# First MoE's second product for two token tiles at once, and a third weight matrix scaled by ScalarE

## The chip, the core and the metric

One core of one Trainium2 chip. The metric is the device time of one launch in microseconds (us), the median of three runs; less is better.

## What is computed

Attention with a bias made from positions, a first MoE layer on its output, and a second MoE layer on that. The reference, cut to what matters here:

```python
x = attention(q, k, v, bias)             # 4 batches, 8 heads, 576 tokens, 64 per head
x = x.transpose(0, 2, 1, 3).reshape(2304, 512)
# first MoE: w_in 512 x 1024, w_out 1024 x 512
h = x @ w_in
solu = h * softmax(h)
ln = (solu - mean(solu)) / sqrt(var(solu) + 1e-6) * g_ln
x = ln @ w_out
# second MoE: w_gate, w_val 512 x 1536, w_out 1536 x 512
out = (sigmoid(x @ w_gate) * (x @ w_val)) @ w_out
```

Inputs come in 8 bytes a number and are decoded on the chip (`decode`). Nearly every product is made of three fp16 products: each factor is split into a high part and a rest (hi, lo), and hi x hi, hi x lo and lo x hi are added up.

## The kernel before

The 2304 tokens are 18 tiles of 128. Attention runs in 72 ticks (`a_qk`, `a_soft`, `a_split`, `a_pv`, `a_x`, `a_xt`): a tick's scores are L553 and L558, its softmax L577 to L596, its transposition a DMA on SP's queue (L601), its product with the values L620. Between ticks the loop over `t` takes up to three items of `side_work`, and from a certain point those come from `moe_items` (L891): for each tile i four quarter-products with w_in (`m_g1`, L767, hps), the softmax and norm (`m_ew1`, `m_ew2`), for the tile before it the transposition into `lt` with its evictions on ScalarE (L812) and VectorE (L813) (`m_ew3`), and four items `m_g2(i - 1, dc)`, dc 0 to 3, for the second product: 24 matmuls of 128 columns each (L824, x2ps <- lt, w1f), weights being a 128 x 128 block of w_out. The item of dc = 3 also evicts the sum (L829 on ScalarE, L830 on VectorE) and stores a tile of 256 KB into the DRAM scratch `x2_d` through SP (L832, x_d <- x). A tile's items may begin only once attention is through with its tokens (`ready`). TensorE's order from `open_moe` to the end of attention is the order of the code (`manual_schedule`); the other engines', and TensorE's later, come from a scheduler with priorities.

After the last tick the rest of the first MoE is interleaved with the second MoE's weights. The weights are units in a list: `w2_dec` loads 512 KB through SP (`load_w`, L690, wraw, three buffers), decodes on VectorE (L184, L185, L188) and squares on ScalarE; `w2_scale(jc)` and `w2_scale_out` make the scales (the latter's out-scale is L1148 and L1150); `w2_split` scales the matrix (L695 on GpSimd, w2tmp <- w2f, sw), takes the high part (L698, ScalarE) and the rest (L699 on GpSimd, w2f <- w2tmp, w2f). Twelve splits of the third matrix (mat 2, w_out) stand behind the out-scale. `load_x2` brings x2 back in groups of 4, 2, 4, 4 and 4 tiles (L1191, xb <- x_d).

Group 0 is computed plainly: `gate_val` for twelve column blocks j makes s_ps (L1342, 512 columns), ScalarE's sigmoid, VectorE's gate product (L1348, fr <- s_ps, fr) and the split of the result for fp16 (L1209 on ScalarE and L1210 on VectorE, gv); `second_out` (L1372, ops) needs gv of all twelve blocks. Group 1 does the same with 256 columns. The last three groups use sums of weight blocks and of x2 blocks (`w2_sums`, `x2_sums`, VectorE's L1228 through the helper `add`, 126 in all, and L1231 on ScalarE) and seven products in place of eight (`seven`, `gate_val7`, prod L1304).

The functions that the change touches:

Of the kernel before, what the change touches and what calls it, by code (L numbers as in the profile page):

```python
# [41 lines left out]
NP = 4  # L42
NP16 = 3
NPT = 4
NLT = 2
SPLIT = 0
NGB = 2
GB_ACT = (0,)
# [1 line left out]
W2A = 12  # L50
W2B = 10
W2P = 0
NHT = 2
NET = 0
TAILQ = 1
BD = 2
# [46 lines left out]
def attn_moe_kernel(  # L103
# [7 lines left out]
    act, dve, pool, pe, sp = nc.scalar, nc.vector, nc.gpsimd, nc.tensor, nc.sync  # L111
# [8 lines left out]

    dram = enter(ctx, "scratch", 1, space=DRAM)
    bias_d = dram.tile([5, 128, H, 640], F32, name="bias_d")
    x2_d = dram.tile([18, 128, 4, 2, 128], F16, name="x2_d")

    const = enter(ctx, "const")
    sm0 = enter(ctx, "sm0", 1)
# [77 lines left out]
    def ring(nm, shape, dt, tag=None):  # L204
        r = rings[nm]
        n = turn.get(nm, 0) % len(r)
        turn[nm] = n + 1
        return r[n].tile(shape, dt, name=nm, tag=tag or nm)
# [481 lines left out]
        sp.dma_start(out=raw.rearrange("p f t -> p (f t)"), in_=src[rows, cols].bitcast(I32))  # L690
        return raw

    def split_w(w, s_, hi, lo, tmp, eng=None):
        if eng is None:
            pool.tensor_scalar(out=tmp, in0=w, scalar1=s_, scalar2=0.0, op0=ALU.mult, op1=ALU.add)  # L695
        else:
            act.activation(out=tmp, in_=w, func=ACTF.Copy, scale=s_)
        act.activation(out=hi, in_=tmp, func=ACTF.Copy)  # L698
        (eng or pool).tensor_tensor(out=lo, in0=tmp, in1=hi, op=ALU.subtract)  # L699
# [103 lines left out]
    def m_ew3(i):  # L803
        mo.pop((i, "m"))
        e = mo.pop((i, "e"))
        lt = glob["lt"].tile([128, 2, 8, 128], F16, name="lt")
        for n in range(2):
            tp = ps_m.tile([128, 4, 128], F32, name="ltp", tag="m")
            for f in range(4):
                pe.transpose(tp[:, f], e[:, 512 * n + 128 * f:512 * n + 128 * f + 128], id_sb)  # L810
            hi = lt[:, 0, 4 * n:4 * n + 4]
            act.activation(out=hi, in_=tp, func=ACTF.Copy)  # L812
            dve.tensor_tensor(out=lt[:, 1, 4 * n:4 * n + 4], in0=tp, in1=hi, op=ALU.subtract)  # L813
        mo[i, "lt"] = lt

    def m_g2(i, dc):
        lt = mo[i, "lt"]
        if dc == 0:
            mo[i, "x2"] = ps_m.tile([128, 4, 128], F32, name="x2ps", tag="m")
        ps = mo[i, "x2"]  # L820
        n = 0
        for f in range(8):
            for (wl, ll) in ((0, 0), (0, 1), (1, 0)):
                pe.matmul(ps[:, dc], wout16[:, f, wl, 128 * dc:128 * dc + 128], lt[:, ll, f],  # L824
                          start=(n == 0), stop=(n == 23))
                n += 1
        if dc == 3:
            x2 = glob["x2"].tile([128, 4, 2, 128], F16, name="x2")
            act.activation(out=x2[:, :, 0], in_=ps, func=ACTF.Copy, scale=2.0 ** -15)  # L829
            dve.scalar_tensor_tensor(out=x2[:, :, 1], in0=ps, scalar=2.0 ** -15, in1=x2[:, :, 0],  # L830
                                     op0=ALU.mult, op1=ALU.subtract)
            glob["st"] = sp.dma_start(out=x2_d[i], in_=x2)  # L832
            mo.pop((i, "lt"))
            mo.pop((i, "x2"))


    ticks, tiles, ready = [], [], []
# [51 lines left out]
            when(u, lambda bb=bb, hp=hp, prep=prep: prep(bb, hp), at if nm == "v" else late)  # L889

    def moe_items():  # L891
        for i in range(19):
            if i < 18:
                for n in range(2):
                    for half in range(2):
                        yield ready[i] + LAG_PV + LAG_X + 1, (lambda i=i, n=n, half=half: m_g1(i, n, half))
                yield 0, (lambda i=i: m_ew1(i))
            if i >= 1:
                yield 0, (lambda i=i: m_ew3(i - 1))
            if i < 18:  # L900
                yield 0, (lambda i=i: m_ew2(i))
            if i >= 1:
                for dc in range(4):
                    yield 0, (lambda i=i, dc=dc: m_g2(i - 1, dc))


    xt_p = {0: enter(att_x, "xt0", 2, "right")}
# [103 lines left out]
    def open_moe():  # L1011
        st.close()
        ms = glob["s"] = ExitStack()
        xt_p[1], xt_p["M"] = enter(m1, "xt1", 2), enter(m1, "xtm", 1)
        glob.update((nm, enter(ms, nm, bufs)) for nm, bufs in
                    (("e", 2), ("hs", 1), ("lt", NLT), ("x2", 1), ("ms", 4)))
        grow("p", NP - NP0)
        grow("p16", NP16 - NP160)
        grow("pt", NPT - NPT0)
        done.add("open")  # L1020
# [105 lines left out]

    def w2_split(mat, jc, c):
        split_w(w2f[mat][:, 4 * jc + c], sw[:, jc, S_G + mat:S_G + mat + 1], w2h16[mat][:, 4 * jc + c, 0],
                w2h16[mat][:, 4 * jc + c, 1], w2t_p.tile([128, 512], F32, name="w2tmp", tag="w2sgn"))

    def w2_scale(jc):
        pow2(w2st, [(4 * jc, 4 * jc + 4)], sw[:, jc, P_G:P_G + 1], sw[:, jc, S_G:S_G + 1], psx[0], 13)
# [37 lines left out]
        glob["e"] = enter(glob["s"], "et", NET)  # L1170
    for _ in range(W2A):
        units.pop(0)()
    seen = glob["st"]
    while side_step(None):
        if glob["st"] is not seen:
            seen = glob["st"]
            with tc.issue_after(seen.ins):
                for _ in range(W2B):
                    if units:
                        units.pop(0)()  # L1180
# [6 lines left out]

    def load_x2(g):
        n, o = sizes[g], first[g]
        t = ring("xb", [128, 4, 4, 2, 128], F16)  # L1190
        sp.dma_start(out=t[:, 0:n], in_=x2_d[o:o + n].rearrange("t p c l q -> p t c l q"))  # L1191
        xb[g] = t

    load_x2(0)
# [9 lines left out]
    def f32t():  # L1204
        return ring(fring[0], [128, 2, 256], F32, "fr")
# [14 lines left out]
    def half_x(xx, nt, kh, th):  # L1220
        def get(l, kk=None):
            if kk is None:
                return xx[:, nt * th:nt * th + nt, 2 * kh:2 * kh + 2, l, :]
            return xx[:, nt * th:nt * th + nt, 2 * kh + kk, l, :]
        return get

    def add(out_, a, b, op=ALU.add):
# [97 lines left out]
    def gate_val(g, n, xx, gvs, js):  # L1325
        nn = 128 * n
        for j in js:
            if j % 4 == 0:
                gvs.append(ring("gv", [128, 2, 4, 512], F16))
            gv, jj = gvs[-1], j % 4  # L1330
            for _ in range(5 if j < 8 else 7):
                if units:
                    units.pop(0)()
            prods = []
            both = ps_s.tile([128, 2, 4, 128], F32, name="s_ps", tag="s_ps")
            for i, w in enumerate(w2h16[:2]):
# [28 lines left out]
    def second_out(g, n, gvs):  # L1365
        for tt in range(n):
# [125 lines left out]
```

## Time and profile before

| | |
|---|---|
| median of 3 runs | 1077.29 us (1076.18 to 1077.48) |
| the profiled execution | 1073.33 us, of which the span of the trace is 1071.6 |
| mean granted TensorE clock | 0.907 |
| TensorE, matmuls (PE) | 898.8 us busy, 84% of the span |
| TensorE, weight loads (PEld) | 634.6 us, 59%; they overlap the matmuls |
| VectorE (DVE) | 769.3 us, 72% |
| ScalarE (ACT) | 618.9 us, 58% |
| GpSimd (POOL) | 426.4 us, 40% |
| chain of work that ended last | TensorE 30%, VectorE 12%, DMA 3% of the span |

Busy times are sums over the whole span; stages with different limits are told apart in the rows below. SP is the engine that issues most DMAs and does so in order.

### The profile page before, as it was taken

To read this page: it belongs to the slowest core of one execution; us is meant where nothing else is said; L and a number is where in the kernel's file an instruction comes from. 1 tells how busy PE (TensorE), PEld (TensorE's weight loads), DVE (VectorE), ACT (ScalarE), POOL (GpSimd) and SP (SyncE) were. 2 spreads that over 40 slices of the span, in tenths; PEclk is the share of its full clock that TensorE was granted. 3 is DMA by queue.
4 is the path that set the end of the run, shared out by engine and by line. 5 is a ranking of instruction groups with operands and counts; after the bars stand their busy time and mean duration, and the time that the engine had idled before them with its cause. 6 is when DMAs were issued, how large, how long until landed. Compare 5 with 4: busy or idle time off the path is not lost.

```text
span 1071.6 us, 23952 instructions
## 1 busy us (share of the span) xinstructions
PE 898.8 (84%) x9566; PEld 634.6 (59%) x9566; DVE 769.3 (72%) x1556; ACT 618.9 (58%) x1283; POOL 426.4 (40%) x386
## 2 busy tenths in 40 slices
PE   2656465668888789989998887798999999999998
PEld 2534344455665566667665664345577856866873
DVE  6879989885576676667664999999954762871760
ACT  4787684767677797778873677744342322331331
POOL 3357555565566666455640487567000000000000
PEclk9656675568899999999999999998999999999999
DMA  7878999899889899999964555500110010001001
GB/s 226 286 231 201 219 242 274 201 239 197 171 177 204 181 196 200 194 205 204 162 123 152 165 158 186 168 24 17 40 40 20 1 60 20 2 1 41 2 1 40
DMA packets 256576, 146.54 MB, mean 137 GB/s; under 512 B 215376, under 2 KB 230992, under 8 KB 256464
## 3 DMA queue, kind: packets, MB, share of 16 engines
q1 hardware_dynamic: 253888, 143.18, 56.4%
q0 software_dynamic: 2048, 1.58, 0.6%
q8 instruction: 75, 1.23, 0.5%
q10 hardware_dynamic: 528, 0.26, 0.1%
q14 instruction: 37, 0.30, 0.1%
HBM read 82.46 MB, written 20.05 MB: 96 GB/s over the span
## 4 chain that ended last, share of the span: by engine, by line
PE 30%; DVE 12%; DMA 3%; issue 2%; POOL 2%; ACT 2%; SPq 0%; POOLq 0%; DVEq 0%; ACTq 0%
PE prod L1304 15%; PE ops L1372 10%; DVE fs L1228 3%; DVE w2f L185 2%; DMA wraw<-in_moe_w_gate_dram 2%; DVE w2f L188 2%; PE x2ps L824 2%; DMA wraw<-in_moe_w_val_dram 1%; POOL w2tmp L695 1%; PE s_ps L1342 1%; PE hps L767 1%; DVE w2s L1228 1%; POOL w2f L699 1%; DVE w2f L184 1%; DMA wraw<-in_moe_w_out_dram 1%
## 5 line engine op out<-in xcount | busy, mean ns | idle before, releaser
L596 POOL TENSOR_TENSOR p<-p,p 128x1024 f16<-128x1024 f32 x72 | 156.2, 2170 | 132.6 <-ACT p L595 89.9
L1228 DVE TENSOR_TENSOR fr<-prod,fr 128x512 f32<-128x512 f32 x126 | 85.0, 687 | 93.8 <-PE prod L1304 92.1
L1372 PE MATMUL ops<-w2f,gv 128*128 128x512 f16 x648 | 144.0, 381 | 4.4 <-POOL w2f L699 2.2
L584 ACT ACTIVATE p<-p,m,sc 128x576 f32<-128x576 f32 x144 | 124.1, 864 | 2.6
L824 PE MATMUL x2ps<-lt,w1f 128*128 128x128 f16 x1728 | 110.0, 224 | 13.9 <-DVE lt L813 11.7
L577 DVE CUSTOM_DVE_ANT_0 p<-score,gk 128x576 f32<-128x576 f32 x144 | 102.9, 750 | 20.9 <-PE score L558 19.3
L824 PEld LDWEIGHTS <-w1f 128*128 128x128 f16 x1728 | 104.3, 100 | 20.9 <-issue 18.6
L1342 PE MATMUL s_ps<-xb,w2f 128*128 128x512 f16 (+1 forms) x576 | 99.9, 332 | 12.7 <-DVE fr L1348 11.2
L1372 PEld LDWEIGHTS <-gv 128*128 128x128 f16 x648 | 63.5, 98 | 79.0 <-issue 5.9
L620 PE MATMUL xps<-gk,pt 128*128 128x64 f16 (+1 forms) x2240 | 88.9, 204 | 17.3 <-DMA pt<-p 17.2
L456 PEld LDWEIGHTS <-mask 128*128 128x128 f16 (+1 forms) x1312 | 65.9, 122 | 55.4 <-issue 20.6
L620 PEld LDWEIGHTS <-pt 128*128 128x128 f16 (+1 forms) x2240 | 83.3, 108 | 25.6 <-DMA pt<-p 18.9
L1304 PEld LDWEIGHTS <-w2f 128*128 128x128 f16 x864 | 84.5, 98 | 11.8 <-issue 1.1
L1342 PEld LDWEIGHTS <-w2f 128*128 128x128 f16 x576 | 57.5, 100 | 53.4 <-issue 11.6
L553 PE MATMUL score<-gk,qt 64*128 64x512 f16 (+1 forms) x480 | 71.0, 429 | 19.8 <-DVE m L577 8.5
L1209 ACT ACTIVATE gv<-fr 128x512 f16<-128x512 f32 (+1 forms) x60 | 34.8, 585 | 84.5 <-DVE fr L1362 70.4
L456 PE MATMUL bp<-rhs,mask 128*128 128x64 f16 (+1 forms) x960 | 53.1, 225 | 29.3 <-DVE gb L482 15.5
L767 PE MATMUL hps<-w1f,xt 128*128 128x512 f16 x312 | 72.6, 379 | 3.1 <-DVE mm L778 1.9
L595 ACT ACTIVATE p<-p 128x1152 f16<-128x1152 f32 x54 | 62.6, 1160 | 11.2 <-DMA pt<-p 9.3
L1304 PEld LDWEIGHTS <-w2s 128*128 128x128 f16 x648 | 63.4, 98 | 7.3
L582 ACT ACTIVATE m<-m,sc 128x1 f32<-128x1 f32 x144 | 40.0, 288 | 46.0 <-DVE m L577 45.7
L767 PEld LDWEIGHTS <-xt 128*128 128x128 f16 x384 | 36.7, 99 | 46.8 <-issue 9.9
(196 smaller groups left out, 1796.8 us busy)
## 6 DMA issues: line engine op xcount, KB each, us to landing
gk<-bias_d SPq DMA_DIRECT2D x24, 576.0 KB
wraw<-in_moe_w_out_dram SPq DMA_DIRECT2D x20, 512.0 KB
wraw<-in_moe_w_gate_dram SPq DMA_DIRECT2D x12, 512.0 KB
wraw<-in_moe_w_val_dram SPq DMA_DIRECT2D x12, 512.0 KB
sraw<-in_q_dram SPq DMA_DIRECT2D x12, 384.0 KB
sraw<-in_k_dram SPq DMA_DIRECT2D x12, 384.0 KB
sraw<-in_v_dram SPq DMA_DIRECT2D x12, 384.0 KB
bias_d<-gk SPq DMA_DIRECT2D x8, 576.0 KB
```

The lines of the kernel that those rows point to most:

```text
L456: pe.matmul(big[0:np_, jj // 8, o:o + 64], lhsT, rhs[i].rearrange("p c h g -> p (c h g)"), start=(i == 0), stop=(i == 1),)
L553: pe.matmul(score[p0:p1, 1024 * hh:1024 * hh + 512], qt[rows, nr * ql + r, p0:p1], KT[bb, hp][rows, 640 * kl:640 * kl + 512], start=(m == ...
L577: dve.tensor_tensor_reduce(out=pp[:, hh], in0=score[:, 960 * hh:960 * hh + S], in1=bi, scale=1.0, scalar=-3.0e38, op0=ALU.add, op1=ALU.max ...
L584: act.activation(out=pp[:, hh], in_=pp[:, hh], func=ACTF.Exp, bias=m[:, 2 + hh:3 + hh], scale=col(C), accum_out=sm[:, c + hh:c + hh + 1])
L596: pool.tensor_tensor(out=p16[:, :, 640:1152], in0=view(pp, 0, [[640, 2], [1, 512]]), in1=view(p16, 0, [[1280, 2], [1, 512]]), op=ALU.subtract)
L620: pe.matmul(o, a, b_, start=(n == 0), stop=(n == len(seq) - 1))
L767: pe.matmul(h, xt[:, xl, kk, off:off + 128], win16[:, 2 * kk + n, wl], start=(kk == 0 and xl == 0 and wl == 0), stop=(kk == 3 and xl == 1),)
L824: pe.matmul(ps[:, dc], wout16[:, f, wl, 128 * dc:128 * dc + 128], lt[:, ll, f], start=(n == 0), stop=(n == 23))
L1228: dve.tensor_tensor(out=out_, in0=a, in1=b, op=op)
L1304: pe.matmul(p[:, jf, 0:nn], w(wl, kk, jf), x(xl, kk), start=(m == 0), stop=(m == 5))
L1342: pe.matmul(ps[:, 0:n], w[:, 4 * (j // 4) + c, wl, o:o + 128], xx[:, 0:n, c, xl, :], start=(m == 0), stop=(m == 11))
L1372: pe.matmul(ps, gvs[j // 4][:, gl, j % 4, 128 * tt:128 * tt + 128], w2h16[2][:, j, wl], start=(m == 0), stop=(m == 35))
```

## The change

The second product of the first MoE takes two tiles at a time. `lt` becomes one tile with three slots; `m_g2(k, dc)` multiplies a weight block with the two slots of pair k, 256 columns in one matmul. The blocks dc 0 and 1 are issued in one step of `moe_items`, dc 2 and 3 in the next step but one tile; each two are evicted together, and the pair's store of 512 KB follows dc 3. Since the slots turn, the two tiles of a pair may come in either order; `placed` keeps it for the output. `x2_d`, `load_x2`, `half_x`, `x2_sums` and `gate_val` follow the new layout. The tail's softmax buffers go from two to one (`NHT`). The third matrix is scaled by ScalarE in place of GpSimd (`scaler`). The units of the weights are taken at every tile's `m_ew3` behind the last store.

```diff
-NLT = 2
-NHT = 2
+NHT = 1
-    x2_d = dram.tile([18, 128, 4, 2, 128], F16, name="x2_d")
+    x2_d = dram.tile([9, 128, 4, 2, 2, 128], F16, name="x2_d")
-    def split_w(w, s_, hi, lo, tmp, eng=None):
-        if eng is None:
+    def split_w(w, s_, hi, lo, tmp, eng=None, scaler=None):
+        if eng is None and scaler is None:
             pool.tensor_scalar(out=tmp, in0=w, scalar1=s_, scalar2=0.0, op0=ALU.mult, op1=ALU.add)
         else:
             act.activation(out=tmp, in_=w, func=ACTF.Copy, scale=s_)
@@ m_ew3
-        lt = glob["lt"].tile([128, 2, 8, 128], F16, name="lt")
+        glob["tile"] = i
+        lt = glob["lt"][:, i % 3]
@@ m_g2
-    def m_g2(i, dc):
-        lt = mo[i, "lt"]
-        if dc == 0:
-            mo[i, "x2"] = ps_m.tile([128, 4, 128], F32, name="x2ps", tag="m")
-        ps = mo[i, "x2"]
+    def m_g2(k, dc):
+        u, v = sorted((2 * k + n) % 3 for n in range(2))
+        turned = 2 * k % 3 != u
+        if dc % 2 == 0:
+            mo[k, "x2"] = ps_m.tile([128, 2, 256], F32, name="x2ps", tag="m")
+        ps = mo[k, "x2"]
         n = 0
         for f in range(8):
             for (wl, ll) in ((0, 0), (0, 1), (1, 0)):
-                pe.matmul(ps[:, dc], wout16[:, f, wl, 128 * dc:128 * dc + 128], lt[:, ll, f],
-                          start=(n == 0), stop=(n == 23))
+                pe.matmul(ps[:, dc % 2].rearrange("p (t q) -> p t q", t=2), wout16[:, f, wl, 128 * dc:128 * dc + 128],
+                          glob["lt"][:, u:v + 1:v - u, ll, f], start=(n == 0), stop=(n == 23))
                 n += 1
...
+        if dc % 2 == 0:
+            return
+        hi, lo = (x2[:, dc - 1:dc + 1, :, l].rearrange("p c t q -> p (c t) q") for l in range(2))
+        ps = ps.rearrange("p c (t q) -> p (c t) q", t=2)
+        act.activation(out=hi, in_=ps, func=ACTF.Copy, scale=2.0 ** -15)
+        dve.scalar_tensor_tensor(out=lo, in0=ps, scalar=2.0 ** -15, in1=hi, op0=ALU.mult, op1=ALU.subtract)
         if dc == 3:
...
+            placed.extend((2 * k, 2 * k + 1)[::-1 if turned else 1])
+            glob["st"] = sp.dma_start(out=x2_d[k], in_=x2)
@@ moe_items
-        for i in range(19):
+        for i in range(20):
...
-            if i >= 1:
+            if i % 2 and i >= 3:
+                for dc in (2, 3):
+                    yield 0, (lambda i=i, dc=dc: m_g2((i - 3) // 2, dc))
+            if 1 <= i <= 18:
                 yield 0, (lambda i=i: m_ew3(i - 1))
             if i < 18:
                 yield 0, (lambda i=i: m_ew2(i))
-            if i >= 1:
-                for dc in range(4):
-                    yield 0, (lambda i=i, dc=dc: m_g2(i - 1, dc))
+            if i % 2 == 0 and i >= 2:
+                for dc in (0, 1):
+                    yield 0, (lambda i=i, dc=dc: m_g2((i - 2) // 2, dc))
@@ w2_split
-                w2h16[mat][:, 4 * jc + c, 1], w2t_p.tile([128, 512], F32, name="w2tmp", tag="w2sgn"))
+                w2h16[mat][:, 4 * jc + c, 1], w2t_p.tile([128, 512], F32, name="w2tmp", tag="w2sgn"),
+                scaler=act if mat == 2 else None)
@@ behind attention
-    seen = glob["st"]
+    seen = glob["tile"]
     while side_step(None):
-        if glob["st"] is not seen:
-            seen = glob["st"]
-            with tc.issue_after(seen.ins):
+        if glob["tile"] != seen:
+            seen = glob["tile"]
+            with tc.issue_after(glob["st"].ins):
                 for _ in range(W2B):
@@ load_x2
-        sp.dma_start(out=t[:, 0:n], in_=x2_d[o:o + n].rearrange("t p c l q -> p t c l q"))
+        for i in range(n // 2):
+            sp.dma_start(out=t[:, i], in_=x2_d[o // 2 + i])
@@ second_out
-            tl = tiles[i]
+            tl = tiles[placed[i]]
```

SP's queue, from the last transposition of attention (pt <- p) to the first of the second MoE's weights (wraw). Before:

```order
L832 DMA x_d<-x_9227 128x1024
L601 DMA_TRANSPOSE pt<-p_9266 128x18x128
L1191 DMA xb<-x_d 128x4x1024
L832 DMA x_d<-x_9516 128x1024
L690 DMA wraw<-in_moe_w_gate_dram 128x1024 x4
L690 DMA wraw<-in_moe_w_val_dram 128x1024 x4
L690 DMA wraw<-in_moe_w_gate_dram 128x1024
```

With the change:

```order
L840 DMA x_d<-x_8390 128x2048
L600 DMA_TRANSPOSE pt<-p_8715 128x18x128
L1204 DMA xb<-x_d 128x2048 x2
L689 DMA wraw<-in_moe_w_gate_dram 128x1024 x4
L689 DMA wraw<-in_moe_w_val_dram 128x1024 x4
L689 DMA wraw<-in_moe_w_gate_dram 128x1024 x2
```

The store that stood between the load of x2 and the first weight load is gone from there.

VectorE behind the out-scale (sw <- sw, sc): fs are sums of weight blocks, fr <- s_ps the gate products, gv the splits of the gate's result. Before:

```order
L1148 SCALAR_TENSOR_TENSOR sw<-sw,sc 128x1 x3
L1150 SCALAR_TENSOR_TENSOR sc<-sc 128x1
L1228 TENSOR_TENSOR fs<-w2f_9623 128x512 x3
L1210 TENSOR_TENSOR gv<-fr,gv 128x512
L1228 TENSOR_TENSOR fs<-fs 128x512
L1228 TENSOR_TENSOR fs<-w2f_9623 128x512
L1228 TENSOR_TENSOR w2s_11818<-fs,w2s_11818 128x512
L1228 TENSOR_TENSOR fs<-fs 128x512
L1348 SCALAR_TENSOR_TENSOR fr<-s_ps,fr 128x512
```

With the change:

```order
L1160 SCALAR_TENSOR_TENSOR sw<-sw,sc 128x1 x3
L1162 SCALAR_TENSOR_TENSOR sc<-sc 128x1
L1361 SCALAR_TENSOR_TENSOR fr<-s_ps,fr 128x512
L1241 TENSOR_TENSOR fs<-w2f_8922 128x512 x3
L1241 TENSOR_TENSOR fs<-fs 128x512
L1223 TENSOR_TENSOR gv<-fr,gv 128x512
L1241 TENSOR_TENSOR fs<-w2f_8922 128x512
L1241 TENSOR_TENSOR fs<-fs 128x512
L1241 TENSOR_TENSOR w2s_10921<-fs,w2s_10921 128x512
```

Behind the out-scale stand now six gate products of 512 columns where there were three (a fourth stood just ahead of it), and six splits where there were four.

VectorE around the last 512-wide split of the gate (gv <- fr, gv 128x512), the last thing that group 0's second_out waits for. Before:

```order
L1348 SCALAR_TENSOR_TENSOR fr<-s_ps,fr 128x512
L1228 TENSOR_TENSOR fs<-fs,w2f_9624 128x512
L1228 TENSOR_TENSOR fs<-fs 128x512
L1348 SCALAR_TENSOR_TENSOR fr<-s_ps,fr 128x256
L1228 TENSOR_TENSOR fs<-w2f_9624,fs 128x512
L1210 TENSOR_TENSOR gv<-fr,gv 128x512
```

With the change:

```order
L1361 SCALAR_TENSOR_TENSOR fr<-s_ps,fr 128x512
L1241 TENSOR_TENSOR fs<-w2f_8923 128x512
L1241 TENSOR_TENSOR w2s_10967<-fs,w2s_10967 128x512
L1241 TENSOR_TENSOR fs<-fs 128x512
L1223 TENSOR_TENSOR gv<-fr,gv 128x512
L1361 SCALAR_TENSOR_TENSOR fr<-s_ps,fr 128x256
```

Between the out-scale and this split VectorE's order has 27 sums before and 46 with the change.

## Rows read from the trace of the kernel before

**Rows 1.** Windows: us, busy PE, PEld, DVE, ACT, POOL, clock, DMA, GB/s.

```profile
290.00:548.00 258.00, 233.13 (x3337) 169.16 (x3337) 174.01 (x438) 206.62 (x459) 146.87 (x131) 0.98 0.96 187
571.30:705.30 134.00, 111.29 (x870) 67.02 (x869) 120.10 (x246) 89.00 (x184) 71.76 (x56) 0.97 0.52 165
705.30:738.70 33.40, 26.75 (x122) 13.04 (x120) 32.69 (x38) 14.12 (x26) 33.33 (x22) 0.85 0.10 32
738.70:1071.60 332.90, 327.22 (x2386) 233.38 (x2384) 197.80 (x320) 97.29 (x163) 3.56 (x3) 1.00 0.06 22
```

**Rows 2.** The page's costliest groups (busy, mean ns | idle before): the second product.

```profile
L824 PE MATMUL x2ps<-lt,w1f 128*128 128x128 f16 x1728 | 110.0, 224 | 13.9 <-DVE lt L813 11.7
...
L824 PEld LDWEIGHTS <-w1f 128*128 128x128 f16 x1728 | 104.3, 100 | 20.9 <-issue 18.6
```

**Rows 3.** TensorE's timeline (start, length, count): a tick, and the last score.

```profile
526.85 0.82 PE L553 MATMUL score<-gk,qt 64*128 64x512 f16 x6
...
529.35 2.84 PE L824 MATMUL x2ps<-lt,w1f 128*128 128x128 f16 x48
532.02 0.98 PE L620 MATMUL xps<-gk,pt 128*128 128x64 f16 x28
532.94 0.82 PE L553 MATMUL score<-gk,qt 64*128 64x512 f16 x6
...
547.74 0.82 PE L553 MATMUL score<-gk,qt 64*128 64x512 f16 x6
```

**Rows 4.** The chain that ended last, in order of time: the seven products.

```profile
809.25 55.18 PE prod L1304 x504
```

**Rows 5.** TensorE's timeline: ticks without first-MoE work, and a first product.

```profile
374.77 0.82 PE L553 MATMUL score<-gk,qt 64*128 64x512 f16 x6 [1.32 <-DVE m L577]
...
377.51 0.82 PE L553 MATMUL score<-gk,qt 64*128 64x512 f16 x6 [0.60 <-ACT qt L292]
...
382.15 0.82 PE L553 MATMUL score<-gk,qt 64*128 64x512 f16 x6 [2.26 <-DVE m L577]
...
404.08 4.05 PE L767 MATMUL hps<-w1f,xt 128*128 128x512 f16 x18
```

**Rows 6.** TensorE's waits, 290 to 548 us: total, times, longest.

```profile
PE ktp L251 <- DMA kv<-in_k_dram: 7.2, 3, 3.8
PE x2ps L824 <- DVE lt L813: 5.8, 6, 2.9
```

**Rows 7.** SP's timeline from the last transposition to the first weight load.

```profile
558.25 2.68 SPq L601 DMA_TRANSPOSE pt<-p  x1
...
569.68 0.38 SPq L1191 DMA_DIRECT2D xb<-x_d  x1
570.22 0.99 SPq L832 DMA_DIRECT2D x_d<-x  x1
571.25 2.49 SPq L690 DMA_DIRECT2D wraw<-in_moe_w_gate_dram  x3
```

**Rows 8.** VectorE's timeline from the out-scale to the last 512-wide split.

```profile
705.04 0.30 DVE L1148 SCALAR_TENSOR_TENSOR sw<-sw,sc 128x1 f32<-128x1 f32 x3
...
705.33 2.30 DVE L1228 TENSOR_TENSOR fs<-w2f 128x512 f32<-128x512 f16 x3
...
714.10 4.22 DVE L1228 TENSOR_TENSOR fs<-w2f 128x512 f32<-128x512 f16 x3
...
728.59 0.89 DVE L1228 TENSOR_TENSOR w2s<-fs,w2s 128x512 f16<-128x512 f32 x1 [0.68 <-ACT w2s L1231]
...
737.98 0.68 DVE L1210 TENSOR_TENSOR gv<-fr,gv 128x512 f16<-128x512 f32 x1
...
756.17 1.88 DVE L1228 TENSOR_TENSOR fs<-w2f 128x512 f32<-128x512 f16 x3
```

**Rows 9.** GpSimd's timeline, same stretch: two scalings, two subtractions.

```profile
711.81 2.85 POOL L695 TENSOR_SCALAR w2tmp<-w2f,sw 128x512 f32<-128x512 f32 x2
714.62 3.15 POOL L699 TENSOR_TENSOR w2f<-w2tmp,w2f 128x512 f16<-128x512 f32 x2
```

More of the change, by code (lines that the diff above doesn't have):

```diff
@@ L813, in m_ew3 @@
             dve.tensor_tensor(out=lt[:, 1, 4 * n:4 * n + 4], in0=tp, in1=hi, op=ALU.subtract)
-        mo[i, "lt"] = lt
-    def m_g2(i, dc):
-        lt = mo[i, "lt"]
-        if dc == 0:
-            mo[i, "x2"] = ps_m.tile([128, 4, 128], F32, name="x2ps", tag="m")
-        ps = mo[i, "x2"]
+    placed = []
+    def m_g2(k, dc):
[4 more added lines that the diff above has]
+        ps = mo[k, "x2"]
         n = 0
@@ L823, in m_g2 @@
             for (wl, ll) in ((0, 0), (0, 1), (1, 0)):
-                pe.matmul(ps[:, dc], wout16[:, f, wl, 128 * dc:128 * dc + 128], lt[:, ll, f],
-                          start=(n == 0), stop=(n == 23))
+                pe.matmul(ps[:, dc % 2].rearrange("p (t q) -> p t q", t=2), wout16[:, f, wl, 128 * dc:128 * dc + 128],
+                          glob["lt"][:, u:v + 1:v - u, ll, f], start=(n == 0), stop=(n == 23))
                 n += 1
-        if dc == 3:
[L828 to L834, printed above, removed]
+        if dc == 0:
+            mo[k, "x"] = glob["x2"].tile([128, 4, 2, 2, 128], F16, name="x2")
+        x2 = mo[k, "x"]
+        if dc % 2 == 0:
[4 more added lines that the diff above has]
+        dve.scalar_tensor_tensor(out=lo, in0=ps, scalar=2.0 ** -15, in1=hi, op0=ALU.mult, op1=ALU.subtract)
+        if dc == 3:
+            placed.extend((2 * k, 2 * k + 1)[::-1 if turned else 1])
+            glob["st"] = sp.dma_start(out=x2_d[k], in_=x2)
     ticks, tiles, ready = [], [], []
@@ L1015, in open_moe @@
         glob.update((nm, enter(ms, nm, bufs)) for nm, bufs in
-                    (("e", 2), ("hs", 1), ("lt", NLT), ("x2", 1), ("ms", 4)))
+                    (("e", 2), ("hs", 1), ("lt", 1), ("x2", 1), ("ms", 4)))
+        glob["lt"] = glob["lt"].tile([128, 3, 2, 8, 128], F16, name="lt")
         grow("p", NP - NP0)
@@ L1189, in load_x2 @@
         n, o = sizes[g], first[g]
-        t = ring("xb", [128, 4, 4, 2, 128], F16)
-        sp.dma_start(out=t[:, 0:n], in_=x2_d[o:o + n].rearrange("t p c l q -> p t c l q"))
+        t = ring("xb", [128, 2, 4, 2, 2, 128], F16)
+        for i in range(n // 2):
+            sp.dma_start(out=t[:, i], in_=x2_d[o // 2 + i])
         xb[g] = t
@@ L1222, in get @@
             if kk is None:
-                return xx[:, nt * th:nt * th + nt, 2 * kh:2 * kh + 2, l, :]
-            return xx[:, nt * th:nt * th + nt, 2 * kh + kk, l, :]
+                return xx[:, th, 2 * kh:2 * kh + 2, :, l, :]
+            return xx[:, th, 2 * kh + kk, :, l, :]
         return get
@@ L1270, in tile_ @@
         def tile_():
-            return f32t().rearrange("p k (t q) -> p t k q", q=128)[:, 0:nt]
+            return f32t().rearrange("p k (t q) -> p k t q", q=128)
         def part(n):
             t = xs_p.tile([128, 2, 2, 2, 128], F16, name=f"x2s{n}")
-            return lambda l, kk=None: t[:, l, 0:nt] if kk is None else t[:, l, 0:nt, kk]
+            return lambda l, kk=None: t[:, l] if kk is None else t[:, l, kk]
         t1, t2, t3, t4 = (part(n) for n in range(4))
@@ L1341, in gate_val @@
                     for (wl, xl) in ((0, 0), (0, 1), (1, 0)):
-                        pe.matmul(ps[:, 0:n], w[:, 4 * (j // 4) + c, wl, o:o + 128], xx[:, 0:n, c, xl, :],
+                        pe.matmul(ps[:, 0:n], w[:, 4 * (j // 4) + c, wl, o:o + 128], xx[:, 0:n // 2, c, :, xl, :],
                                   start=(m == 0), stop=(m == 11))
```

## The prediction

> **What bounds the kernel now.** I read the windows view first, stage by stage, because the page's busy shares average over stages with different limits. Up to 548 us attention runs, with the first MoE of earlier tokens between its ticks: there TensorE is the fullest engine, 233.13 of 258.00 us [rows 1]. From 571.30 to 705.30 the second MoE's weights are loaded, decoded, squared and scaled: VectorE is busy 120.10 of 134.00 us. From 705.30 to 738.70 VectorE is full (32.69 of 33.40) and so is GpSimd (33.33), while TensorE has 26.75. From 738.70 to the end TensorE is full, 327.22 of 332.90. So a saving on TensorE counts before 548 us and after 738.70 us, and one on VectorE between.
>
> The changed product lies mostly in the first stage. The page puts 110.0 us of TensorE on its 1728 matmuls [rows 2]; those durations are latencies that overlap. TensorE's timeline gives the price: 48 of 128 columns in 2.84 us, 2.67 of it until the next work starts, so 55.8 ns each [rows 3]. A tick there lasts from 526.85 to 532.94 us, which is its scores, these 48 and the attention product, without a gap. The stretch of 504 matmuls of 256 columns took 55.18 us [rows 4], or 109.5 ns each.
>
> **The change, part by part.** The sum is made against the profiled execution, 1073.33 us; the median of the runs shown, 1077.29, is 3.96 above it, and I add that at the end.
>
> *Matmuls merged.* 1728 x 55.8 = 96.4 us become 864 x 109.5 = 94.6. Halving the weight loads (104.3 us of loads, mean 100 ns [rows 2]) gives nothing: they overlap, and a matmul of 128 columns already costs half of one of 256. Of it, 1104 were issued before the last score: 61.6 - 60.4 = **-1.2 us**.
>
> A rule speaks for more: the Trainium skill, "TensorE: Matmul & The Clock Gate", section "Back-to-back issue gap", has a sustained stream of load and matmul pairs at 128 columns at about 81 ns a matmul. By its figure the 1104 would cost 89.4 us and the gain would be some 29; the trace disagrees, with 55.8 ns over 48.
>
> *Attention up to the last score (A).* Counting the orders: by the last score one more tile has had its first product on TensorE, 24 matmuls of 512 columns (18 take 4.05 us, so 0.22 each [rows 5]): **+5.2**. With two tiles' product in four blocks over two steps, the work between ticks is spread otherwise: ticks with no first-MoE matmul rise from 4 to 10. In three of these TensorE now waits 1.32, 0.60 and 2.26 us [rows 5], 1.4 on average, so six more cost **+8.4** (bounds 3.6 and 13.6). Against that, TensorE's other waits before 548 us can take up such shifts: 5.8 us for the transposed tile and 7.2 for a load of keys and values [rows 6]; I take half of each, **-6.5** (bounds 0 and -13.0). Sum **+5.9**.
>
> Then the handover. The last score stands at 547.74 [rows 3]; the first load of the second MoE's weights is issued at 571.25, 23.5 us later, behind the last transposition (558.25, 2.68 us), the load of x2 (569.68) and a store (570.22) [rows 7]. SP works in order, so that store's wait holds the weights. Now no store stands between the load of x2 and the weights, and TensorE has 24 wide matmuls and 18 of the first product left where it had 144 and 24. What stays is 10.5 us from last score to transposition, 2.7 of transposition, about 1 for the last attention product and about 2 to land and store: 16 us. **-7.5** (from 0, if a late tile still holds SP's load of x2, to -9.5 without the landing). A is **-1.6** in all; I keep -11 and +6 as its ends.
>
> *Weights (B), 571 to 705.* The order puts four fewer operations of 512 on VectorE before the out-scale (three gate products and two splits fewer, one larger eviction more): 4 x 0.65 (between 0.60 and 0.68, [rows 8]) = **-2.6**. The shorter store list (three of 512 KB for six of 256 KB among the weight loads) moves the same bytes; SP's queue at 0.52 of DMA's time has room [rows 1]. One buffer of the tail's softmax less costs nothing: VectorE's order already had the earlier tile's use first.
>
> *Scaling moved from GpSimd to ScalarE, and what VectorE now does first (C).* This is the term that decides. The out-scale stands at 705.04 and the first VectorE work behind it at 705.33; the last 512-wide split of the gate ends at 738.66 [rows 8]: 33.3 us. second_out cannot take a tile before that split, since it sums over all twelve column blocks. In that stretch VectorE has 27 weight sums, 4 splits, 3 gate products of 512 and one of 256. Now it has 46 sums, 6 splits and 6 products: 58 for 34 of 512. Plain, one takes 0.68 and three 1.88, so 0.60 from start to start [rows 8]. So 34 x 0.60 + 0.33 = 20.7 now, one wait of 0.7, and 11.9 lost beside GpSimd's 11 scalings and 10 subtractions of the third matrix. Beside a pair of subtractions (3.15 us [rows 9]) three sums took 4.22 for 1.88: 1.17 lost for each subtraction, the upper end. Shared evenly over the 21 operations it is 0.57, the lower end. I take 0.79: the scalings cost something as well, for the three sums beside a pair of them (705.33) took 2.30, but less. ScalarE now does the scaling, with only 14.12 of its 33.40 us taken [rows 1]; GpSimd is left with 12 subtractions. After: 58 x 0.60 = 34.8, 12 x 0.79 = 9.5, 0.7 of wait, together 45.0: **+11.7** (bounds 12 x 0.57 and 12 x 1.17: +9.0 and +16.2; +6 if VectorE gets ahead of the subtractions).
>
> Here a rule is to be weighed. The trace shows sums at 0.77 us each beside a pair of scalings and at 1.41 beside a pair of subtractions [rows 8]. The Trainium skill, "SBUF — State Buffer", says that the port pair of VectorE and GpSimd is an exclusive lock against any GpSimd operation that reads SBUF when VectorE has two SBUF inputs; by it scalings would cost as much as subtractions and C would be 2.6 us lower, at the lower end above; the trace so far bears it out in part.
>
> *TensorE to the end (D).* Behind that split TensorE had 332.9 us with almost no slack [rows 1]. Now 19 more gate matmuls of 256 columns come after it (2.1 us), less some 0.6 of waits that ScalarE's scaling removes: **+1.5** (0 to +4).
>
> Sum: -1.6 - 2.6 + 11.7 + 1.5 = **+9.0**. Profiled 1082.3, median **1086.3**.
>
> **The rivals.** *Faster: attention ends early.* The ticks without first-MoE work cost nothing more, since ScalarE and VectorE catch up within the tick behind them, all the waits of rows 6 go, and the weights start 11 us sooner; C comes out at +8 with the splits beside ScalarE's scaling. -11 - 2.6 + 8 = -5.6: 1071.7. It decides as soon as A is below C's cost. For it: the 23.5 us of rows 7. Against it: the waits of the empty ticks [rows 5].
>
> *Nothing: the change doesn't do what it says.* Columns set TensorE's price, the sums of VectorE are the same 126 in all, and the order of the gate's work is made good by TensorE's idle 6.65 us between 705.30 and 738.70 [rows 1]. Then only the -1.2 and a little more are left: -1.5, 1075.8.
>
> *A single pace of loads.* If a load and its matmul had one price whatever the columns, the 1104 would be halved: -30.8 us, 1046.5; [rows 4] deny it, with 109.5 ns against 55.8. [...]
>
> *Heavier: the last pair comes late.* A pair is evicted and stored only when both tiles are through; the last one's store stands ahead of two of the loads of the out-weights, which wait in SP's order behind it. With A at +6 and C at +16.2 it is 1077.3 - 2.6 + 22.2 + 1.5 = 1098.
>
> **How the numbers follow.** My forecast 0.54, faster 0.23, nothing 0.14, one pace 0.02, heavier 0.07. A measurement here can tell 0.2% (2.2 us) from no change. Faster: the faster rival, the single pace, and a little of the nothing case: 0.27. Same: most of the nothing case: 0.12. Slower: 0.61. The forecast's own range is 1079 to 1095, by the bounds of A, C and D, not all at one end. To leave out no more than 2 in 10 it has to reach the faster case: 1070 to 1096.
>
> **What would show it.** The tick with these matmuls should still last about 6.1 us, with 24 matmuls of 256 columns in some 2.6. The first weight load should be issued some 16 us after the last score, at about 570. From the out-scale to the last 512-wide split should be about 45 us, with VectorE at over 95% and GpSimd idle between its subtractions. TensorE should then be full to the end, for about 334 us. If the first weight load comes before 562, or the stretch behind the out-scale stays at 36 us or less, the forecast is wrong; so it is if the wide matmuls take less than 100 ns.

## The result, and the profile after

The changed kernel takes 1090.2 us in the median of 4 runs (1087.43 to 1093.55) against 1076.74 for the kernel before in the same comparison: a ratio of 1.013, with a 95% interval of 1.0097 to 1.0164. It is slower by about 13.5 us. Forecast were 9.0, a median of 1086.3 in a range of 1070 to 1096, which holds the result.

The profiled execution took 1093.55 us, 20.2 more than the one of before. I cut both at the same events: the scores of the fiftieth tick from the end (about where the first MoE begins), the last score, the first load of the second MoE's weights, the out-scale, and the end of group 0's last 512-wide split. The windows view of the change between them (columns as in [rows 1]):

```profile
259.46:561.14 301.68, 267.35 (x3119) 183.77 (x3119) 195.52 (x501) 232.63 (x515) 174.37 (x154) 0.95 0.89 180
561.14:579.83 18.69, 15.10 (x207) 10.82 (x205) 7.68 (x19) 7.67 (x16) 7.28 (x6) 0.91 0.46 102
579.83:716.42 136.59, 100.38 (x600) 60.78 (x602) 120.98 (x238) 86.58 (x180) 73.02 (x56) 0.90 0.51 162
716.42:762.18 45.76, 40.42 (x191) 19.03 (x189) 45.72 (x63) 27.52 (x47) 22.91 (x12) 0.93 0.07 24
762.18:1091.80 329.62, 324.66 (x2379) 232.50 (x2376) 185.18 (x302) 95.41 (x157) 0.00 (x0) 1.00 0.06 22
```

The same view of the kernel before:

```profile
255.02:547.74 292.72, 259.60 (x3647) 187.57 (x3646) 193.13 (x492) 227.97 (x509) 168.31 (x151) 0.97 0.95 186
547.74:571.25 23.51, 20.47 (x336) 16.75 (x334) 12.16 (x29) 11.87 (x23) 11.27 (x10) 1.00 0.49 90
571.25:705.04 133.79, 111.08 (x870) 66.93 (x869) 119.84 (x242) 88.74 (x184) 71.76 (x56) 0.97 0.52 165
705.04:738.66 33.62, 26.97 (x122) 13.18 (x121) 32.90 (x40) 14.34 (x26) 33.28 (x22) 0.85 0.10 32
```

Stretch by stretch: +9.0 us in the 50 ticks, -4.8 at the handover, +2.8 in the weights, +12.1 from out-scale to split, and 329.6 against 332.9 us to the end, -3.3. That makes +15.8, from one execution of each kernel; the medians differ by 13.5. The other 4.4 of the 20.2 lie before the first of these ticks, at 259.46 against 255.02. The first matmul of the first MoE, some 6 us earlier, is as late already (253.2 against 248.8), and the twelve experiments have that tick between 253.7 and 257.0, so this one execution of the change was late there.

Behind the out-scale VectorE is busy 45.72 of 45.76 us. In its timeline there, a sum and a split take 1.65 and 1.64 us while GpSimd subtracts, where they take 0.69 later ([rows 8] for before):

```profile
717.39 1.89 DVE L1241 TENSOR_TENSOR fs<-w2f 128x512 f32<-128x512 f16 x3
719.19 1.65 DVE L1241 TENSOR_TENSOR fs<-fs 128x512 f32<-128x512 f32 x1
720.76 1.64 DVE L1223 TENSOR_TENSOR gv<-fr,gv 128x512 f16<-128x512 f32 x1
...
760.89 0.69 DVE L1241 TENSOR_TENSOR fs<-fs 128x512 f32<-128x512 f32 x1
761.49 0.69 DVE L1223 TENSOR_TENSOR gv<-fr,gv 128x512 f16<-128x512 f32 x1
```

TensorE's timeline prices the merged (wide) matmul: 48 of 256 columns run from 507.37 to 512.61, 109 ns each, as in [rows 4].

```profile
507.37 5.40 PE L826 MATMUL x2ps<-lt,w1f 128*128 128x256 f16 x48
512.61 0.98 PE L619 MATMUL xps<-gk,pt 128*128 128x64 f16 x28
```

SP's timeline at the handover shows the store gone from between the load of x2 and the weights ([rows 7]):

```profile
572.15 2.67 SPq L600 DMA_TRANSPOSE pt<-p  x1
578.99 0.80 SPq L1204 DMA_DIRECT2D xb<-x_d  x2
579.83 11.29 SPq L689 DMA_DIRECT2D wraw<-in_moe_w_gate_dram  x4
```

### The profile page after: what moved, and what is told of

It reads as the page before. It is cut to its first block, busy times and chain, and to the rows that moved or that the text cites. A ratio compares the mean times of both kernels' runs of the same rounds, so it can differ in the third digit from the quotient of the medians.

```text
span 1091.8 us, 22218 instructions
## 1 busy us (share of the span) xinstructions
PE 904.6 (83%) x8701; PEld 626.1 (57%) x8702; DVE 770.1 (71%) x1556; ACT 629.0 (58%) x1295; POOL 415.5 (38%) x374
## 5 line engine op out<-in xcount | busy, mean ns | idle before, releaser
L595 POOL TENSOR_TENSOR p<-p,p 128x1024 f16<-128x1024 f32 x72 | 158.8, 2206 | 146.7 <-ACT p L594 97.5
L1355 PE MATMUL s_ps<-xb,w2f 128*128 128x512 f16 (+1 forms) x576 | 103.4, 339 | 31.4 <-DVE fr L1361 19.4
L619 PE MATMUL xps<-gk,pt 128*128 128x64 f16 (+1 forms) x2240 | 91.7, 207 | 26.5 <-DMA pt<-p 25.6
L826 PE MATMUL x2ps<-lt,w1f 128*128 128x256 f16 x864 | 101.7, 277 | 7.5 <-ACT lt L812 3.7
L619 PEld LDWEIGHTS <-pt 128*128 128x128 f16 (+1 forms) x2240 | 86.7, 110 | 35.0 <-DMA pt<-p 27.5
L826 PEld LDWEIGHTS <-w1f 128*128 128x128 f16 x864 | 85.6, 100 | 18.6 <-issue 4.7
L552 PE MATMUL score<-gk,qt 64*128 64x512 f16 (+1 forms) x480 | 73.5, 443 | 23.0 <-DVE m L576 12.9
L698 POOL TENSOR_TENSOR w2f<-w2tmp,w2f 128x512 f16<-128x512 f32 x36 | 58.4, 1637 | 39.5 <-ACT w2f L697 39.2
```

What stands on the lines that cost most here:

```text
L552: pe.matmul(score[p0:p1, 1024 * hh:1024 * hh + 512], qt[rows, nr * ql + r, p0:p1], KT[bb, hp][rows, 640 * kl:640 * kl + 512], start=(m == ...
L595: pool.tensor_tensor(out=p16[:, :, 640:1152], in0=view(pp, 0, [[640, 2], [1, 512]]), in1=view(p16, 0, [[1280, 2], [1, 512]]), op=ALU.subtract)
L619: pe.matmul(o, a, b_, start=(n == 0), stop=(n == len(seq) - 1))
L826: pe.matmul(ps[:, dc % 2].rearrange("p (t q) -> p t q", t=2), wout16[:, f, wl, 128 * dc:128 * dc + 128], glob["lt"][:, u:v + 1:v - u, ll, ...
```

## The experiments

All twelve are timed against the kernel before, which stood between 1074.3 and 1076.0 in the four comparisons. The stretches, in us of one profiled execution each, lie between the same events as above: the last 50 ticks up to the last score, the handover from there to the first weight load, the weights up to the out-scale, from there to group 0's last split, and from there to the end.

| kernel | median, ratio (95%) | 50 ticks | handover | weights | to split | to end |
|---|---|---|---|---|---|---|
| before | 1076.74 | 292.7 | 23.5 | 133.8 | 33.6 | 332.9 |
| the change | 1090.20, 1.0130 (1.0097 to 1.0164) | 301.7 | 18.7 | 136.6 | 45.8 | 329.6 |
| e1 change, sums late | 1080.16, 1.0038 (1.0017 to 1.0059) | 300.8 | 18.6 | 137.0 | 29.9 | 337.5 |
| e2 before, sums late | 1067.67, 0.9926 (0.9901 to 0.9951) | 292.0 | 23.5 | 131.8 | 19.5 | 338.9 |
| e3 change, GpSimd scales | 1090.23, 1.0132 (1.0109 to 1.0155) | 300.4 | 17.5 | 135.2 | 48.3 | 330.5 |
| e4 before, ScalarE scales | 1073.21, 0.9985 (0.9965 to 1.0005) | 293.7 | 23.7 | 134.8 | 33.3 | 330.8 |
| e5 e1 in 22 items | 1051.30, 0.9791 (0.9761 to 0.9822) | 282.2 | 20.5 | 132.0 | 22.7 | 338.1 |
| e6 e1, 128 columns | 1064.58, 0.9915 (0.9884 to 0.9946) | 301.6 | 17.5 | 128.3 | 21.6 | 337.7 |
| e7 e1, one step | 1096.17, 1.0184 (1.0154 to 1.0213) | 315.9 | 17.4 | 136.5 | 28.1 | 337.9 |
| e8 e2, ScalarE scales | 1063.91, 0.9892 (0.9866 to 0.9918) | 295.0 | 24.0 | 131.0 | 18.2 | 337.3 |
| e9 change in 22 items | 1059.75, 0.9849 (0.9823 to 0.9876) | 281.1 | 20.4 | 131.1 | 37.2 | 329.4 |
| e10 before in 18 items | 1078.14, 1.0018 (0.9998 to 1.0037) | 299.6 | 18.1 | 134.0 | 32.0 | 334.8 |
| e11 e1 in 26 items | 1079.82, 1.0032 (1.0016 to 1.0047) | 277.7 | 25.0 | 137.7 | 46.1 | 337.1 |
| e12 e5, 128 columns | 1056.18, 0.9826 (0.9797 to 0.9855) | 284.8 | 20.9 | 127.8 | 24.7 | 338.2 |

### e1 and e2: the weight sums behind the gate

The sums were to be issued behind the out-scale; now they are issued behind group 0's last split, in the change (e1) and in the kernel before (e2):

```diff
             split_gv(sg, gv, jj, 0, nn)
+            if g == 0 and j == 11:
+                glob["so"] = glob["lo"]
@@ split_gv
-        dve.tensor_tensor(out=lo, in0=y, in1=hi, op=ALU.subtract)
+        glob["lo"] = dve.tensor_tensor(out=lo, in0=y, in1=hi, op=ALU.subtract)
```

> The change, but the weight sums may be issued only behind the last 512-wide split of group 0's gate, not behind the out-scale. Theory (VectorE's sums in front of the gate's rest cost the time): VectorE's order has 12 operations between out-scale and that split, not 58, so the 45.5 us there fall to what TensorE needs for its 125 gate matmuls of 512 (27 us) and a few waits, about 32; the sums then run beside TensorE's later work, and the time falls by some 10 to 13 us, to 1077 to 1080. Rival (that stretch is bound by TensorE or ScalarE anyway, or the sums then come late for the seven products): within 3 us of the change's 1090.

> The kernel before with the same edit. Theory: 7 operations in place of 34 stand between out-scale and last split, so the 33.3 us there fall towards TensorE's own work in it (26.8 us busy) and GpSimd's splits of the third matrix are the next limit for second_out; 4 to 7 us less than before, 1070 to 1073. Rival (the sums are needed in time by the seven products, or GpSimd's splits hold the end): no change, 1075 to 1079.

e1 is 10.0 us below the change, e2 8 us below the kernel before: the theory holds for both, and e2 went further than forecast. The windows of e1:

```profile
712.79:742.64 29.85, 29.85 (x152) 14.66 (x150) 9.20 (x17) 21.42 (x37) 14.26 (x12) 1.00 0.07 22
742.64:1080.10 337.46, 332.17 (x2416) 236.18 (x2414) 211.36 (x349) 100.89 (x168) 0.00 (x0) 1.00 0.06 22
```

The stretch falls from 45.8 to 29.9 us, and its bound changes: VectorE has 9.20 us left and TensorE is busy all the time. Some 8 us come back behind it, since TensorE now does there what it did beside the sums. What is left in the stretch goes with the gate's matmuls of 512 columns that TensorE still has behind the out-scale, at 0.22 us each: the 117 of e1 are 25 us of its 29.9, the 64 of e2 and e8 14 of 19.5 and 18.2, the 80 of e6 17 of 21.6, the 185 of e11 40 of 46.1.

### e3 and e4: who scales the third matrix

e3 is the change with `scaler=None`; e4 is the kernel before with `scaler=act if mat == 2 else None` and nothing else of the change.

> The change with the third matrix scaled by GpSimd again. Theory (the scaling's move is not what puts the sums ahead; the later gate is): VectorE's order still has 43 sums, 6 products and 6 splits between out-scale and last split; GpSimd's 12 scalings come back beside them, so 2 to 6 us slower than the change, 1092 to 1096. Rival (the move of the scaling let VectorE's sums in ahead): 1078 to 1081, most of the loss undone.

> The kernel before with only the third matrix's scaling moved to ScalarE. Theory: VectorE keeps 29 sums, 4 splits and 3 products between out-scale and last split, and GpSimd no longer scales beside them; 2 to 6 us less in that stretch, time 1071 to 1075. Rival (the move by itself costs): 1085 or more.

e3 stands at the change's time, and e4's interval takes in the time of before. The rivals are out: VectorE's order has 43 sums ahead of the last split in e3, 46 in the change, so the moved scaling did not put them there. In e3 the stretch is 2.5 us longer, but the time did not follow: forecast were 1092 to 1096. e4's median lies within its theory's 1071 to 1075, but not by that theory: the stretch was to lose 2 to 6 us and lost 0.3. In it lie 36 operations of VectorE beside 12 subtractions, where 34 lay beside 11 scalings and 10 subtractions.

### e5, e9 and e11: the pace of the items

Each block of 24 wide matmuls is given out in two items (e5; e9 with the sums as in the change), or in three (e11):

```diff
-    def m_g2(k, dc):
+    def m_g2(k, dc, part=None):
...
-        n = 0
-        for f in range(8):
+        n = 12 if part == 1 else 0
+        for f in {None: range(8), 0: range(4), 1: range(4, 8)}[part]:
...
+        if part == 0:
+            return
@@ moe_items, and likewise for (0, 1)
                 for dc in (2, 3):
-                    yield 0, (lambda i=i, dc=dc: m_g2((i - 3) // 2, dc))
+                    for part in range(2):
+                        yield 0, (lambda i=i, dc=dc, part=part: m_g2((i - 3) // 2, dc, part))
```

> The kernel of e1, with each block of 24 wide matmuls given out as two items of 12, so that a pair of tiles is 22 items between the ticks as before the change, not 18. Theory (fewer items let the first MoE run up to the tokens that attention has not made yet, leave ticks without its matmuls, and pack the rest behind them): by the last score TensorE's order has 312 first and 504 second-product matmuls, not 336 and 552, and the last score comes at 545 to 551, not 557 to 561; part of the 9 us comes back at the handover, as more is left. Time 3 to 7 us below e1's 1080, 1073 to 1077. Rival (TensorE's work is the same and only its place differs): within 2 us of e1.

> The change with each block given out as two items of 12 matmuls, as in e5, but the weight sums issued behind the out-scale again, as in the change. Theory (pace and sums are two separate losses): the last score stays at about 536 as in e5, against 557 to 561; between out-scale and last split VectorE has 36 sums, 4 products and 5 splits, 45 x 0.60 + 9.5 = 37 us against e5's 23, of which some 5 come back behind; time 8 to 12 us above e5's 1051, 1059 to 1063. Rival (only the two together give the 29 us): 1070 or more.

> The kernel of e5 with three items for each block (9, 9 and 6 matmuls), 26 items for a pair. Theory (the fewer first-MoE matmuls stand before the last score, the sooner it comes): 288 first and 480 second-product matmuls before it, three ticks without any: last score at 526 to 533; but the handover grows, and 8 gate products are left behind the out-scale in place of 4, some 8 us more there; time within 6 us of e5's 1051. Rival (22 items were only luck, more of them put work back behind attention): 1060 or more.

e5 did far more than forecast: 1051.3, 29 us below e1 and 2.1% below the kernel before; it is the best of the study. The windows of e5, e11 and e1 over the 50 ticks, each from its own kernel's view:

```profile
254.05:536.24 282.19, 252.08 (x3047) 174.21 (x3047) 194.62 (x491) 227.11 (x507) 169.83 (x151) 0.96 0.95 191
```

```profile
256.70:534.42 277.72, 245.93 (x2992) 168.59 (x2991) 189.28 (x478) 221.96 (x498) 168.20 (x150) 0.96 0.95 192
```

```profile
256.40:557.20 300.80, 268.00 (x3120) 184.85 (x3120) 195.88 (x501) 232.32 (x515) 174.17 (x154) 0.94 0.90 181
```

TensorE is idle 30.1, 31.8 and 32.8 us in the three, but busy 252.1, 245.9 and 268.0. The pace sets how much of the first MoE is put before the last score, and the last score waits for it. In the 18.6 us e5 gains there on e1, 15.9 are busy time. Some 10 of these are 24 matmuls of 512 and 48 of 256 columns that e5 has not issued by then; the rest goes with the clock: 30.7 us of e1's busy time there lie at a granted clock of one half (1.2 GHz), 19.1 of e5's, and a matmul takes twice as long there (256 columns start 213 ns apart, not 109). Behind the last score e5 gives 1.9 us back at the handover and gains 5.0 in the weights and 7.2 to the split, with 87 gate matmuls left behind the out-scale for e1's 117. e9 against e5 prices the sums apart from the pace: 8.5 us of median, the stretch 37.2 against 22.7 (forecast 37 against 23), and 8.7 of it given back behind. e11 goes too far, as its rival said: work kept out of attention comes back at the handover (25.0 us) and as eight gate blocks behind the out-scale (46.1).

### e10: the change's pace in the kernel before

Two blocks of 128-column matmuls are one item, nothing else:

```diff
-                for dc in range(4):
-                    yield 0, (lambda i=i, dc=dc: m_g2(i - 1, dc))
+                for dc in (0, 2):
+                    yield 0, (lambda i=i, dc=dc: (m_g2(i - 1, dc), m_g2(i - 1, dc + 1)))
```

> The kernel before with two blocks of 24 matmuls of 128 columns in one item, so that two tiles are 18 items, not 22; nothing merged, stores and sums as before. Its order has the change's ten ticks without first-MoE matmuls, and 336 first and 1152 second-product matmuls before the last score. Theory (the pace of items costs the attention, not the merged matmul): last score at 555 to 562, not 548 to 550, handover short as in the change (17 to 20 us, not 23.5); in all 2 to 6 us slower than before, 1077 to 1081. Rival (the merging itself or its buffers cost the attention): last score within 2 us of 549, time within 2 us of before.

The last score stood at 553.5, 1.5 us short of what was forecast; but the 50 ticks took 299.6 us against 292.7 before, 6.9 of the 9.0 that they cost in the change, and the handover fell to 18.1. Its windows row and TensorE's first waits:

```profile
253.94:553.49 299.55, 268.52 (x3728) 194.43 (x3728) 199.24 (x502) 228.94 (x513) 175.99 (x154) 0.95 0.89 183
```

```profile
PE score L553 <- DVE m L577: 10.1, 7, 2.8
PE ktp L251 <- DMA kv<-in_k_dram: 8.5, 2, 5.9
```

TensorE's waits for the softmax of a tick grow to 10.1 us, from 4.2 in the kernel before (8.5 in the change), but its idle time in all does not: 31.0 us against 33.1. What grows is the work before the last score, 268.5 against 259.6: 24 matmuls of 512 columns more at 0.22 us and 48 of 128 at 0.056 are 7.9 of these 8.9. The whole costs 2.2 us (interval -0.2 to +4.0), so pace alone is not the change's loss.

### e6, e12 and e7: merging, and the two steps

e6 and e12 put two matmuls of 128 columns in place of each merged one. e7 issues all four blocks of a pair in one step.

```diff
@@ e6
-                pe.matmul(ps[:, dc % 2].rearrange("p (t q) -> p t q", t=2), wout16[:, f, wl, 128 * dc:128 * dc + 128],
-                          glob["lt"][:, u:v + 1:v - u, ll, f], start=(n == 0), stop=(n == 23))
+        for t, s in enumerate((u, v)):
...
+                    pe.matmul(ps[:, dc % 2, 128 * t:128 * t + 128], wout16[:, f, wl, 128 * dc:128 * dc + 128],
+                              glob["lt"][:, s, ll, f], start=(n == 0), stop=(n == 23))
@@ e7
-            if i % 2 and i >= 3:
-                for dc in (2, 3):
-                    yield 0, (lambda i=i, dc=dc: m_g2((i - 3) // 2, dc))
...
-                for dc in (0, 1):
+                for dc in range(4):
                     yield 0, (lambda i=i, dc=dc: m_g2((i - 2) // 2, dc))
```

> The kernel of e1, with every matmul of 256 columns replaced by two of 128, one for each tile of the pair; items, evictions and stores as they are. Theory (columns set the price, 55.8 ns against 109.5): 1104 for 552 before the last score, so the last score 0 to 2 us later than e1's and the time within 2 us of e1's 1080. Rival (halving the loads pays): 5 us or more slower than e1.

> The kernel of e5 with matmuls of 128 columns again: each block's two items are now the 24 matmuls of one tile and the 24 of the other. Pairs, evictions, stores, sums and the pace of 22 items stay. Theory (the pace and the place of the work make e5's gain, the merging next to none of it): from tick to tick as in e5, 281 to 285 us from 255 us to the last score at 535 to 540, and the time within 4 us of e5's 1051. Rival (the merged matmul carries it): 290 us or more to the last score, 1059 or more.

> The kernel of e1, with all four blocks of a pair in one step of the item list, not two and two. Theory: ticks without first-MoE matmuls are the same ten and the items are as few, so the last score stays at 556 to 561 and the time within 3 us of e1's 1080. Rival (the halves over two steps are what the attention pays for): last score at 550 or earlier, 1075 or less.

Up to the last score the forecast of e6 and e12 held: 301.6 against 300.8 us, and 284.8 against 282.2 (e12's last score stood at 540.8, forecast were 535 to 540). The merging is worth 1 to 3 us there, by one execution of each. But e6's time missed both theories: 15.6 us below e1, all of it behind attention, where the scheduler made another order. Eight of the twelve gate blocks precede the out-scale, not six, and the weights take 128.3 us, not 137.0. In e1's weights stage TensorE waits for the gate products of VectorE, which stand behind decoding in its order, 22.6 us in two waits; in e6 the longest waits of the gate's matmuls for VectorE are 6.8 and 5.9 us. e12 is 4.9 us above e5, just over the 4 that the theory allowed. e7 missed both theories too: 315.9 us for the 50 ticks. Behind the softmax of a tick, TensorE waits there most for a tile's own norm and transposition:

```profile
PE score L552 <- DVE m L576: 8.3, 7, 2.7
PE x2ps L826 <- DVE mm L792: 7.6, 2, 4.6
PE ltp L810 <- POOL e L800: 7.3, 5, 2.0
```

The change waited 1.2 us for the last of them, and the second is not among its first eleven. So the halves over two steps cost nothing; they save some 15 us against all four at once.

e8 (e2 with ScalarE scaling) came out as its theory had it:

> The kernel of e2 (before, with the sums behind the gate's last split) and the third matrix scaled by ScalarE. Theory: between out-scale and last split nothing of VectorE's 7 operations lies beside GpSimd's scalings any more, and second_out's wait for the splits of the third matrix goes; 0 to 4 us below e2's 1067.7, 1064 to 1068. Rival (ScalarE's gate work is then held up by the scalings): 1070 or more.

At 1063.91 it is 3.8 us below e2, the intervals of the two ratios overlapping.

## Why the prediction was right, and where not

**Attention to the last score (A, first part): +5.9 forecast, +9.0 measured.** The terms were right, but one was missing. TensorE's busy time grew by 7.8 us (267.35 against 259.60), of which the step had 4.0, the 24 matmuls of the first product less the merging. The idle time grew by 1.2; the step had 1.9, as +8.4 for empty ticks and -6.5 for waits that go (the waits for a tick's softmax grew by 4.3). The step priced every matmul at the full clock, but the granted clock fell from 0.97 to 0.95: 28.8 us of the busy time lie at 1.2 GHz, before 18.2. At half the pace the 10.6 us more cost some 5.3, and the work itself grew by about 2.5. The ten ticks without first-MoE matmuls, in which TensorE is often idle, lie in these two windows of the change:

```profile
352.10:380.90 28.80, 18.22 (x249) 13.39 (x246) 21.36 (x42) 22.97 (x52) 18.93 (x18) 0.82 0.84 182
454.40:473.10 18.70, 13.36 (x219) 9.00 (x218) 10.51 (x29) 13.53 (x34) 10.49 (x9) 0.82 1.07 206
```

The three profiles with this order on TensorE (the change, e1, e3) have 28.8 to 31.5 us busy at 1.2 GHz, the four with the order of before (before, e2, e4, e8) 17.3 to 22.4. Yet e6 and e10, with the same ten ticks, have 18.8 and 19.9, so what sets the clock there is open. e6 is busy 3.7 us less than e1 and waits 4.5 more, and its stretch is as long:

```profile
256.24:557.79 301.55, 264.29 (x3672) 191.23 (x3672) 196.04 (x501) 232.06 (x515) 173.06 (x154) 0.97 0.89 180
```

e10 shows that the pace of items by itself comes to 6.9 us without any merging, and e5 that it can be turned into a gain.

**The handover (A, second part): -7.5 forecast, -4.8 measured.** The store between the x2 load and the weights is gone (0.8 us from one to the other, before 1.6 [rows 7]), and the load of x2 follows the last transposition by 6.8 us, not 11.4. The step allowed 2 us for landing and store and 1 for the last product. So A in all was +4.2 and not -1.6: the sum of A failed, through TensorE's busy time before the last score and the longer handover.

**Weights (B): -2.6 forecast, +2.8 measured.** The count of VectorE's operations was right, the step's premise not. The decoding's three groups took 88.4 us of VectorE in place of 85.5, and two waits came in: 2.2 us for a sigmoid and 1.4 for a product of TensorE in the chain to the out-scale. TensorE was idle 36.2 us there, before 22.7; its longest waits in the change:

```profile
PE s_ps L1355 <- DVE fr L1361: 14.1, 1, 14.1
PE s_ps L1355 <- DVE sw L167: 9.1, 1, 9.1
```

The order in which the scheduler mixes gate and decoding is the likely cause, though not shown by itself: e6, which differs from e1 in the matmuls' size and in that order, has 128.3 us for e1's 137.0, more than the whole miss. Why the scheduler chose as it did was not tried, nor were the single softmax buffer, the stores of two tiles and the new place of the weights' units tried by themselves.

**Sums ahead of the gate (C): +11.7 forecast, +12.1 measured.** This was the term that decided, and e1 and e9 show it. The 58 operations were there, 34.8 us at 0.60; from the first of them at 716.78 to the split's end they took 45.4, so 10.6 were lost, all beside GpSimd's 12 subtractions, where the step had 9.5 and a wait of 0.7.

**TensorE to the end (D): +1.5 forecast, -3.3 measured.** The step put 19 matmuls of group 1 more behind the split; the trace has 256 there, before 254. And it left out the products of second_out, whose sums end behind the split but begin ahead of it: 40 of their matmuls of 512 columns now lie ahead, before 29, so 608 are left in place of 619, 2.4 us less. The windows of those matmuls alone (ops: us, PE, ACT, clock, DMA, GB/s), before and with the change:

```profile
738.66:1071.60 332.94, 135.40 (x619) 12.31 (x18) 1.00 0.06 22
762.18:1091.80 329.62, 133.02 (x608) 12.33 (x18) 1.00 0.06 22
```

TensorE's idle time fell from 5.7 to 5.0 us besides. Between out-scale and split it was busy 40.42 us, before 26.97, mostly with 60 gate matmuls that stood in the weights stage before.

The faster rival failed: counted from the first of the 50 ticks the weights started 4.1 us later, not 11 sooner. The rival that nothing happens failed at its last condition: the gate's order was not made good by idle TensorE. The single pace of loads fell as [rows 4] said. By an estimate from the figure of the Trainium skill's "TensorE: Matmul & The Clock Gate", section "Back-to-back issue gap", about 81 ns for a matmul of 128 columns, e6's 552 extra matmuls before the last score would have cost some 29 us; the measured stretch grew by 0.8, and at 2.4 GHz e6's matmuls of 128 columns start 56 ns apart. The heavier rival needed A at +6 and C at +16.2; A came to +4.2, C to +12.1. A miss of 5.8 in A and 5.4 in B was partly met by one of -4.8 in D, which was luck, so the sum came nearer than its terms.

## What to carry to other kernels

Where one stage's order comes from counting items between ticks, a change that merges items also changes the pace, and with it how much work stands before a stage's last step; keep the number of items, or set it on purpose. Where a scheduler fills an engine with whatever is ready, work that is needed late gets ahead of the path's last steps: read the order for what stands before the one operation that the next engine waits for, and tie the rest behind it. Check the price of a column before merging matmuls: if half the columns cost half the time, little is saved. And look at the granted clock before a longer busy time is taken for more work.

## What was not expected of the hardware

Beside GpSimd, two operations price differently. e3 has 12 scalings beside VectorE that the change has not. With 55 operations, 33.0 us at 0.60, it lost 14.9 us of 47.9 there; the change lost 10.6 beside the 12 subtractions alone. A scaling thus cost VectorE some 0.36 us, a subtraction 0.88. Where the time lost is put down to the GpSimd operation beside which it fell, the kernel before has 0.34 and 0.76, e3 0.36 and 0.86. By the Trainium skill's "SBUF — State Buffer", section "SBUF: two separate sides", both should hold the shared port pair alike against sums with two SBUF inputs; here the measured cost of a scaling is less than half. That the kernel before, with no change, ran from 1071.79 to 1080.98 us in one comparison of 23 runs was wider than the three runs at the start had led me to think, and is why a single profile's 20.2 us overstated the change by half.
